# Adding two of a pair's three word tiles by DMA, with one list of tiles for words and exponentials

## The chip, the cores and the metric

The kernel runs on one core of one Trainium2 chip. The metric is the device time of one execution in microseconds; lower is better. Three runs of the kernel before gave 1370.07, 1371.21 and 1372.68 us, median 1371.21.

## What is computed

Two identical layers of a small transformer, on 2048 tokens of width 512, in bf16, with 32 heads of 16 columns. Each layer is attention and then a dense block with ReLU, each with a residual; the two layers share their weights.

```python
def _A_ref(x, wqkv, wo):
    ...
    scores = jnp.einsum("bhqd,bhkd->bhqk", q, k) * (Dh ** -0.5)
    p = _softmax(scores, axis=-1)
    o = jnp.einsum("bhqk,bhkd->bhqd", p, v)
    return (lambda x, *d: x.transpose(*d))(o, 0, 2, 1, 3).reshape(B, S, D) @ wo

def _B_ref(x, w1, w2):
    h = jnp.einsum("bsd,df->bsf", x, w1)
    ...
    return jnp.einsum("bsf,fd->bsd", h, w2)

x = A_x
x = x + _A_ref(_layernorm(x, axis=-1), A_wqkv, A_wo)
x = x + _B_ref(_layernorm(x, axis=-1), B_w1, B_w2)
x = x + _A_ref(_layernorm(x, axis=-1), A_wqkv, A_wo)
x = x + _B_ref(_layernorm(x, axis=-1), B_w1, B_w2)
```

The scores of both layers are 2 x 32 x 2048 x 2048 numbers, and each needs an exponential.

## The kernel before

**Slots.** A unit of work is 512 score columns: one head (or two or four blocks of keys, where fewer queries are taken), 128 keys on the partitions, queries along the columns. A slot takes W = 3 units. TensorE writes their scores into one of two PSUM tiles `ps_s` of three banks (L1946), and ScalarE turns them into exponentials in bf16, in an SBUF tile `e` (L1959). There are 1365 slots. The value matmuls (`pv`, L1299) multiply these tiles by the values `vaug`, which carry a column of ones for the softmax's denominator, and add up in PSUM `ps_o` or `ps_f`. They use 32 columns of the array each, so four heads run side by side; four such matmuls are called a round here. Between them TensorE does the projections and the dense block, the other matmuls (L429, L657, L666).

**Blocks on VectorE.** In some slots the third unit is not exponentiated by ScalarE, whose instruction then has 1024 columns and not 1536. VectorE evacuates it into the int16 tile `lin` (L1478): scores, a bias added and clamped, whose bits read as bf16 come near to an exponential. Two such blocks make a pair, 1024 columns. For a pair GpSimd makes two more tiles with a 64-bit integer add (L1533): `up` is lin plus a constant in each 16-bit word, `down` is lin minus it. The exponential is taken as lin + up + 1.55 x down. The sum is not formed: TensorE does three value matmuls, of lin and of up with `vaug`, and of down with `vscaled`, the values times 1.55 (for six blocks of keys; elsewhere VectorE weighs the down tile itself, L1537).

```python
            for part, buf, key, of in (
                ("lin", lin[which], line_key, None),
                ("up", up[p["n"] % NC], p["key"] + ("up",), None),
                ("down", down[p["n"] % ND], p["key"] + ("down",), p),
            )
```

So a block on VectorE costs TensorE three value matmuls, and a block on ScalarE one. Six tiles `lin`, three `up`, four `down` and five `e` of 1536 columns are taken in turn.

**The order.** Nothing is scheduled by the compiler. A loop over slots in the kernel's own program keeps a clock for each engine (`now_pe`, `now_dve`, `now_pool`, `exp_end`), with a cost for each kind of work, and writes the instructions of all engines in the order that follows: it picks the units of a slot, decides whether one goes to VectorE (`dve_block`, then `chain` for the pair), fills TensorE's time up to the next scores with value rounds (`fill_v`, `v_round`) and other matmuls (`fill_pe`), and repeats the scores where time is left. Engines then run their lists in order and wait on semaphores. The dictionary `rule` holds thresholds of these choices, `RULES` changes them at given slots, and `STARTS`, `MORE` and `SLIP` override single choices; these are "the table".

**Transfers.** SyncE (`SP`) issues nearly all DMAs: inputs, weights of the dense block (`load_w1`), transposes of the normalised rows (L796), the query tiles (L937) and the small ones of the softmax's denominators (L1191, L1195, L1243). GpSimd issues 46 DMAs that spread a denominator's rows over partitions (`widen`, L1253), and two loads at the start (L212).

Of the kernel before, what the change touches and what calls it, by code (L numbers as in the profile page):

```python
# [26 lines left out]
def kernel(  # L27
# [31 lines left out]
    NE = 5  # L59
# [13 lines left out]
    NP = 6  # L73
    NC = 3
    ND = 4
# [18 lines left out]
    STARTS, MORE, SLIP = {27: 0, 33: 0, 22: 0, 38: 1, 52: 0, 57: 0, 61: 0, 79: 0, 98: 0, 100: 1, 103: 1, 107: 1, 128: 1, 136: 0, 158: 1, 193: 0, 220: 1, 239: 0, 221: 0, 260: 1, 242: 1, 251: 0, 249: 0, 305: 1, 301: 1, 325: 1, 323: 1, 351: 0, 368: 1, 366: 0, 392: 1, 401: 1, 402: 0, 418: 0, 405: 1, 438: 1, 456: 0, 477: 1, 516: 0, 505: 1, 533: 1, 526: 0, 595: 1, 659: 0, 642: 0, 681: 0, 693: 0, 710: 0, 708: 0, 740: 1, 753: 0, 755: 1, 746: 0, 749: 0, 769: 0, 765: 1, 799: 1, 806: 0, 815: 1, 830: 1, 838: 0, 829: 0, 869: 1, 866: 0, 873: 1, 880: 0, 883: 0, 881: 1, 907: 1, 902: 0, 953: 0, 960: 0, 985: 0, 991: 0, 1026: 0, 1046: 0, 1068: 0, 1079: 0, 1067: 1, 1076: 1, 1096: 0, 1128: 0, 1125: 0, 1126: 0, 1156: 0, 1158: 0, 1178: 1, 1164: 0, 1189: 0, 1254: 1, 1280: 0, 1370: 0}, {8: 1.0, 2: -1.0, 15: -1.0, 28: 2.0, 42: -1.0, 80: 2.0, 72: -1.0, 95: 1.0, 92: 1.0, 87: -1.0, 156: 1.0, 166: -1.0, 207: 2.0, 223: 2.0, 234: -1.0, 287: 2.0, 318: -1.0, 407: 1.0, 437: 2.0, 495: -1.0, 486: 2.0, 520: 2.0, 533: 1.0, 564: 1.0, 572: 2.0, 577: 1.0, 594: -1.0, 589: 2.0, 599: -1.0, 620: 2.0, 624: 2.0, 649: -1.0, 660: 2.0, 643: 2.0, 669: -1.0, 683: -1.0, 712: 2.0, 736: 2.0, 735: 2.0, 738: 1.0, 741: 2.0, 758: 2.0, 757: 1.0, 786: 2.0, 784: 1.0, 814: 2.0, 819: 1.0, 839: 1.0, 861: 1.0, 874: 1.0, 865: -1.0, 886: 1.0, 897: 1.0, 892: 2.0, 953: 2.0, 955: 1.0, 941: 1.0, 1000: -1.0, 1022: 2.0, 1028: 2.0, 1033: 1.0, 1061: 1.0, 1119: -1.0, 1117: -1.0, 1112: 1.0, 1181: 1.0, 1205: -1.0, 1220: 1.0, 1221: -1.0, 1241: -1.0, 1255: -1.0, 1250: -1.0, 1276: 2.0, 1281: -1.0, 1326: 1.0, 1335: 2.0, 1357: 2.0, 1341: 2.0, 1347: 2.0}, {54: 216.0, 82: -200.0, 141: 216.0, 168: -200.0, 176: 120.0, 180: -200.0, 194: 120.0, 221: 120.0, 249: 120.0, 241: 216.0, 247: 60.0, 279: 120.0, 278: -200.0, 277: 216.0, 282: 216.0, 309: 120.0, 329: 120.0, 355: 216.0, 377: 120.0, 409: 120.0, 432: 120.0, 524: -200.0, 547: 216.0, 552: 216.0, 544: 120.0, 580: 216.0, 616: 60.0, 612: -200.0, 603: -200.0, 644: 60.0, 722: 120.0, 723: -200.0, 730: 60.0, 777: 120.0, 766: 60.0, 763: 60.0, 784: 216.0, 785: -200.0, 792: 216.0, 803: 60.0, 815: 60.0, 819: -200.0, 835: -200.0, 825: 216.0, 830: -200.0, 887: -200.0, 918: -200.0, 909: 216.0, 903: 216.0, 946: 216.0, 951: 120.0, 958: -200.0, 991: 60.0, 1044: 216.0, 1042: -200.0, 1057: 120.0, 1069: 120.0, 1071: 216.0, 1073: 60.0, 1111: 60.0, 1159: 60.0, 1200: 120.0, 1187: 60.0, 1196: 216.0, 1216: 120.0, 1238: 60.0, 1298: 120.0, 1313: 60.0, 1315: -200.0, 1304: -200.0, 1344: 120.0, 1362: -200.0, 1373: 120.0, 1365: 120.0}  # L94
# [4 lines left out]
        "backlog": 3000.0, "soon": 1400.0, "calm": 9.0, "most": 50.0, "unit": 320.0, "fill": 3000.0,  # L99
        "rounds": 4, "partial": 3, "far": 3, "young": 3, "old": 5, "slack": 1300.0, "eager": 0,  # L100
        "haste": 2.0, "margin": 130.0,
    }
    RULES = {1: {'pressed': 5, 'young': 6}, 21: {'backlog': 4000.0}, 41: {'unit': 360.0, 'pressed': 3, 'hold': 4, 'over': 0.0, 'calm': 1.5, 'cap': 10.0, 'fill': 2000.0, 'rounds': 4}, 61: {'full': 3}, 81: {'unit': 280.0, 'cap': 6.0, 'late': 99.0, 'spare': 10}, 101: {'slack': 300.0, 'fill': 2000.0}, 121: {'margin': 160.0, 'most': 2.0}, 141: {'eager': 0, 'hold': 4, 'late': 3.0, 'rounds': 3, 'pressed': 5, 'margin': 130.0, 'over': 0.0, 'partial': 3}, 161: {'full': 2}, 181: {'full': 2, 'ahead': 3.0, 'calm': 2.0, 'pace': 1.5, 'unit': 320.0, 'partial': 3, 'least': 0.5, 'most': 2.0}, 201: {'far': 2, 'pressed': 3, 'most': 2.0, 'least': 0.5, 'easy': 1.2, 'calm': 3.0, 'near': 8, 'rounds': 4}, 221: {'spare': 20, 'ahead': 3.0, 'calm': 1.2, 'haste': 2.0, 'hold': 4, 'pace': 1.3, 'cap': 3.0, 'young': 4}, 241: {'hold': 4, 'most': 50.0, 'ahead': 5.0, 'haste': 3.0}, 261: {'pressed': 5}, 281: {'cap': 3.0, 'least': 1.0, 'margin': 100.0, 'full': 2}, 301: {'far': 3, 'late': 99.0, 'pressed': 4, 'cap': 3.0, 'backlog': 2200.0, 'calm': 9.0, 'eager': 1, 'unit': 360.0}, 321: {'backlog': 2200.0, 'far': 3, 'eager': 0, 'cap': 6.0, 'unit': 320.0, 'over': 60.0, 'calm': 2.0, 'spare': 14}, 361: {'easy': 1.0, 'late': 2.0}, 381: {'cap': 3.0, 'slack': 300.0}, 401: {'eager': 0, 'pace': 0.7}, 421: {'calm': 9.0, 'old': 4}, 441: {'partial': 2, 'cap': 6.0, 'calm': 1.0, 'fill': 3000.0}, 461: {'pressed': 5}, 481: {'easy': 2.0, 'rounds': 3, 'cap': 10.0, 'pace': 1.0}, 501: {'haste': 1.6, 'ahead': 1.0, 'slack': 300.0, 'least': 1.0}, 521: {'margin': 100.0, 'unit': 360.0}, 541: {'cap': 3.0}, 561: {'closing': 3, 'full': 4}, 581: {'young': 6}, 621: {'partial': 2, 'late': 4.0}, 641: {'ahead': 3.0, 'calm': 1.0}, 661: {'far': 4, 'backlog': 3000.0}, 681: {'calm': 1.2, 'soon': 2000.0, 'unit': 360.0, 'hold': 2, 'far': 2, 'easy': 1.2, 'eager': 1, 'full': 3}, 701: {'young': 4, 'hold': 4}, 721: {'least': 1.0, 'pace': 0.7, 'backlog': 4000.0, 'fill': 3000.0}, 761: {'hold': 2, 'full': 3, 'closing': 6, 'haste': 2.0}, 821: {'over': 120.0, 'partial': 4}, 861: {'pace': 1.5, 'rounds': 3}, 881: {'spare': 6, 'far': 4}, 901: {'backlog': 3000.0}, 941: {'young': 3, 'pace': 1.0, 'far': 4, 'backlog': 3000.0, 'slack': 800.0, 'late': 99.0, 'partial': 2, 'pressed': 5}, 981: {'far': 4, 'slack': 800.0}, 1021: {'ahead': 8.0, 'pace': 0.7, 'rounds': 4, 'near': 6, 'far': 2, 'late': 2.0, 'backlog': 1500.0, 'full': 2}, 1041: {'margin': 60.0, 'young': 4}, 1061: {'margin': 100.0}, 1101: {'old': 4}, 1121: {'rounds': 4}, 1161: {'late': 99.0}, 1201: {'unit': 360.0, 'most': 50.0, 'calm': 1.5, 'over': 200.0, 'full': 4, 'least': 0.5, 'closing': 0, 'cap': 10.0}, 1221: {'margin': 160.0}, 1241: {'calm': 9.0, 'unit': 320.0}, 1261: {'hold': 4}, 1281: {'over': 120.0, 'backlog': 2200.0, 'least': 1.0, 'late': 99.0}, 1301: {'pace': 1.0, 'least': 0.5}, 1321: {'pressed': 4, 'slack': 1300.0}, 1341: {'calm': 1.2, 'unit': 320.0, 'far': 2, 'fill': 2000.0}, 1361: {'slack': 1300.0}}
# [22 lines left out]
    def sb(shape, dt, name):  # L126
# [11 lines left out]
    x_t = [sb([P, D], BF16, f"x{tt}") for tt in range(NTT)]  # L138
# [3 lines left out]
    kt1 = sb([P, 2, QS], BF16, "ktp1_0")  # L142
    ktp = [
# [3 lines left out]
                kt1[:, j, :] if T == 0 and j < 2 else sb([P, QS], BF16, f"ktp1_{T}_{j}")  # L147
# [5 lines left out]
    va2 = [sb([P, 2, H // 2, PW], BF16, f"vaug0_{n}") for n in range((NKB - TPC) // 2)]  # L153
# [3 lines left out]
    ]  # L157
    vaug.append(
        [sb([P, H // 2, PW], BF16, f"vaug1_{kb}") for kb in range(NKB - TPC)] + vaug[0][NKB - TPC :]
# [11 lines left out]
    acc = [  # L171
        x[:].bitcast(FP32).rearrange("p a b -> p (a b)") for x in kt01 + kt2
    ] + [
        x[:].rearrange("p k h d -> p (k h d)")[:, 0 : 2 * QS].bitcast(FP32) for x in va2
    ]
# [339 lines left out]
    def do_task(t):  # L515
# [11 lines left out]
        for k in t["makes"]:  # L527
            if k not in made:
                mark(k, t["engine"])

    def run_act():

        for t in act_q:
# [358 lines left out]
    def v_group(l, kb):  # L892
        def fin(b):
            nc.vector.tensor_copy(out=v_out(l, kb), in_=v_in(b))
            mark(("v", l, kb))
            if l == 0 and kb in SCALED:
                scale_v(l, kb, [])
# [1297 lines left out]
```

## Time and profile before

| | |
|---|---|
| median of three runs | 1371.21 us |
| the profiled execution's own time | 1371.6 us |
| its span, first to last instruction | 1369.8 us |
| granted TensorE clock | 1.000 |
| exponentials (L1959) of 1024 and 1536 columns | 1200 and 165 |
| evacuations of blocks on VectorE (L1478) | 1200, busy 802.4 us |
| adds on GpSimd (L1533) | 1200, busy 735.7 us |

The profile shows one execution. PE is TensorE's matmuls, PEld its weight loads, DVE VectorE, ACT ScalarE, POOL GpSimd, SP SyncE; a name that ends in q is that engine's sequencer. Busy times are in us, the mean of one instruction in ns. A group's line gives source line, engine, operation, tiles written and read, shape and count, then the busy time and mean, then the idle time of the engine just before these instructions and what ended most of it. A line of the waits reads: who waited, for whom, us in total, times, the longest. A line of transfers ends with the median us from issue to landing.

### The profile page before, as it was taken

The numbers are of one execution on the slowest core, as the hardware profiler recorded it, in microseconds if no ns is written. First come the engines' busy times: TensorE is split into PE (matmuls) and PEld (weight loads), VectorE is DVE, ScalarE is ACT, GpSimd is POOL, SyncE is SP. The second block draws the span as 40 slices with busy tenths as digits, with TensorE's granted clock in tenths as the row PEclk, the third lists the DMA queues.
The fourth block names the chain that finished last, engine by engine and source line by source line (L and its number), as shares of the span: only waits on it lengthen the run. The fifth ranks groups of instructions, "written<-read, shape, count | busy, mean of one in ns | idle before, by whom it ended". The sixth has DMA issues, their size and how long they took to land. (4 is left out here: it accounts for less than half of the span.)

```text
span 1369.8 us, 48788 instructions
## 1 busy us (share of the span) xinstructions
PE 1333.9 (97%) x20647; PEld 470.5 (34%) x20647; DVE 1145.0 (84%) x1994; ACT 1344.5 (98%) x1437; POOL 765.7 (56%) x1296
## 2 busy tenths in 40 slices
PE   8999999999999999999999999999999999999998
PEld 3222222222222222222222222222234444545665
DVE  7898998869998889986898877998988886887774
ACT  8999999999999999999999999999999999999995
POOL 3456666546566655664566544565545555565441
PEclk9999999999999999999999999999999999999999
DMA  6200012101022100210111100002112211214120
GB/s 148 70 2 14 21 43 45 47 16 33 11 49 48 23 21 6 56 42 18 25 21 32 33 5 6 11 15 52 41 35 51 50 28 38 65 30 96 35 58 19
DMA packets 151579, 50.03 MB, mean 37 GB/s; under 512 B 136608, under 2 KB 148576, under 8 KB 151360
## 3 DMA queue, kind: packets, MB, share of 16 engines
q1 hardware_dynamic: 144832, 41.31, 13.4%
q0 software_dynamic: 5568, 5.15, 2.0%
q8 instruction: 161, 2.64, 0.8%
q10 hardware_dynamic: 960, 0.46, 0.1%
q14 instruction: 58, 0.48, 0.1%
HBM read 24.38 MB, written 2.10 MB: 19 GB/s over the span
## 5 line engine op out<-in xcount | busy, mean ns | idle before, releaser
L1959 ACT ACTIVATE e<-ps_s 128x1024 bf16<-128x1024 f32 (+1 forms) x1366 | 1330.2, 1172 | 6.9 <-PE ps_s L1946 5.1
L1478 DVE TENSOR_SCALAR lin<-ps_s 128x512 int16<-128x512 f32 x1200 | 802.4, 684 | 154.8 <-PE ps_s L1946 116.5
L1533 POOL INT64_ADD up<-lin x600 | 367.6, 617 | 425.6 <-DVE lin L1478 220.7
L1946 PE MATMUL ps_s<-q,ktp 32*128 32x512 bf16 (+2 forms) x5460 | 523.3, 321 | 12.5 <-ACT e L1959 7.6
L1533 POOL INT64_ADD down<-lin x600 | 368.1, 617 | 130.8 <-DVE lin L1478 46.8
L1946 PEld LDWEIGHTS <-ktp 32*128 32x128 bf16 x5728 | 166.5, 91 | 509.4 <-issue 501.1
L1299 PEld LDWEIGHTS <-vaug 128*32 128x32 bf16 x7338 | 178.6, 95 | 196.0 <-issue 167.1
L1299 PE MATMUL ps_o<-e,vaug 128*32 128x512 bf16 (+2 forms) x2094 | 201.3, 321 | 2.6 <-DVE ht L1163 0.8
L1299 PE MATMUL ps_f<-e,vaug 128*32 128x512 bf16 (+2 forms) x1922 | 198.3, 330 | 1.4 <-DVE q L914 0.8
L1299 PE MATMUL ps_f<-lin,vaug 128*32 128x512 bf16 (+2 forms) x766 | 113.8, 332 | 0.1
L1299 PE MATMUL ps_f<-down,vscaled 128*32 128x512 bf16 (+2 forms) x728 | 113.5, 329 | 0.0
L1299 PE MATMUL ps_f<-up,vaug 128*32 128x512 bf16 (+2 forms) x766 | 113.1, 332 | 0.0
L1299 PE MATMUL ps_o<-up,vaug 128*32 128x512 bf16 (+2 forms) x850 | 110.2, 322 | 0.0
L1299 PE MATMUL ps_o<-lin,vaug 128*32 128x512 bf16 (+2 forms) x850 | 105.6, 322 | 0.5 <-DVE ht L1161 0.3
L1299 PE MATMUL ps_o<-down,vscaled 128*32 128x512 bf16 (+2 forms) x798 | 104.7, 320 | 0.0
L1299 PEld LDWEIGHTS <-vscaled 128*32 128x32 bf16 x1526 | 66.8, 96 | 29.2 <-issue 22.0
L429 PE MATMUL ps_o<-w,ht 128*32 128x512 bf16 x896 | 75.4, 383 | 0.6 <-issue 0.5
L429 PE MATMUL ps_f<-w,ht 128*32 128x512 bf16 x784 | 64.5, 383 | 0.2 <-DVE r L1187 0.2
L429 PE MATMUL ps_f<-xnT,w 128*32 128x512 bf16 x688 | 56.6, 383 | 1.5 <-DVE xn L933 1.2
L429 PE MATMUL ps_o<-xnT,w 128*32 128x512 bf16 x656 | 54.1, 383 | 0.1
L429 PEld LDWEIGHTS <-ht 128*32 128x32 bf16 x1680 | 36.5, 95 | 42.8 <-issue 34.8
L429 PE MATMUL ps_o<-xnT,wkq 128*32 128x512 bf16 x496 | 42.7, 383 | 1.7 <-DVE ht L991 0.5
(181 smaller groups left out, 851.9 us busy)
## 6 DMA issues: line engine op xcount, KB each, us to landing
w<-in_B_w_dram SPq DMA_DIRECT2D x144, 128.0 KB
q<-xn SPq DMA_DIRECT2D x36, 64.0 KB
out_dram<-x SPq DMA_DIRECT2D x15, 128.0 KB
x<-in_A_x_dram SPq DMA_DIRECT2D x14, 128.0 KB
ktp<-in_B_w_dram SPq DMA_DIRECT2D x10, 128.0 KB
r<-u POOLq DMA_DIRECT2D x8, 128.0 KB, 4.6
u<-u POOLq DMA_DIRECT2D x8, 128.0 KB, 4.6
xnT<-xn SPq DMA_TRANSPOSE x55
```

Source lines behind the costliest of these rows:

```text
L429: nc.tensor.matmul(G["b"][cols], lhsT[:, cols], rhs, start=not G["begun"][g], stop=not G["cols"][g], tile_position=(0, 32 * g), skip_group ...
L1299: nc.tensor.matmul((ps_f, ps_o)[sg["bank"]][32 * g : 32 * g + 32, 0 : sg["w"]], values[:, 4 * sg["T"] + g, 2 * e : 2 * e + 32], rhs, start ...
L1478: first = nc.vector.tensor_scalar(out=lin[which][:, half * QS : (half + 1) * QS], in0=src, scalar1=EXP_BIAS, scalar2=THIRD, op0=ALU.add, o ...
L1533: nc.gpsimd.int64_add(words(out), words(line), by)
L1946: score = nc.tensor.matmul(b[:, a : a + sg["w"]], kt[32 * g : 32 * g + 32, kc : kc + P], q_home(sg["q"])[32 * g : 32 * g + 32, sg["e"], 0 ...
L1959: ex = nc.scalar.activation(out=eb[:, 0 : place[m]], in_=b[:, 0 : place[m]], func=ACTF.Exp, scale=1.0 / (LOG2E * UNIT),)
```

## The change

- A pair can be *joined*: GpSimd issues a DMA that adds the pair's lin tile to its up tile in place (bf16), and TensorE multiplies that sum and the down tile, two value matmuls a block and not three. Whether a pair is joined is decided by `joins`: where GpSimd's queue reaches no further ahead than `rule["join"]`. The built program has 380 such transfers for 629 pairs.
- lin, up and down tiles, and exponential tiles too, come from one list `words` of 16 tiles of 1024 columns, taken when a task is written and given back after the last reader; ScalarE writes most 1024-wide exponentials there, and keeps three 1536-wide tiles (`NE`) of its own. Up to seven slots may be pending (`MOST`) in place of five.
- Tiles that a stage does not need are lent to that list and taken back later: `w2`, `wo`, `wv` and the key half of `wkq`, rows of `x`, keys and values of the second layer before they exist. What was overwritten is loaded again by SyncE before use (35 loads of w2, 40 of wo, 8 of wv, 4 of x).
- The first layer's first queries go through their keys in another order of runs, one matmul at the start is left out, and the table is new.

```diff
-    NE = 5
+    NE = 3
...
-    NP = 6
-    NC = 3
-    ND = 4
+    NWORDS = 16
+    X_BACK, W2_BACK, WO_BACK = 15, 5, 15
+    MOST = 7
...
+    JOINING, ADDED = 950.0, 3900.0
+    JOIN = {}
...
-    STARTS, MORE, SLIP = ...
+    STARTS, MORE, SLIP = ...
...
-    lin = [sb([P, GROUP * QS], I16, f"lin{n}") for n in range(NP)]
-    up = [sb([P, GROUP * QS], I16, f"up{n}") for n in range(NC)]
-    down = [sb([P, GROUP * QS], I16, f"down{n}") for n in range(ND)]
+    words_two = [sb([P, 2 * GROUP * QS], I16, f"words{n}") for n in range(NWORDS // 2)]
+    words = [
+        words_two[n // 2][:, n % 2 * GROUP * QS : (n % 2 + 1) * GROUP * QS] for n in range(NWORDS)
+    ]
+    free_words = list(range(NWORDS))
...
+    lent_w = [lend(wv[:, 2 * n : 2 * n + 2, :].rearrange("p c f -> p (c f)")) for n in range(2)]
...
+    lent_w2 = [
+        lend(w2[:, 2 * n : 2 * n + 2, :].rearrange("p a f -> p (a f)")) for n in range(NF // 2)
+    ]
...
-            steps = [(0, range(4), 0, TPC), (0, range(4), TPC, 2 * TPC), (0, range(4), 2 * TPC, NKB)]
+            steps = [(0, range(4), 0, TPC), (0, range(MID), TPC, 2 * TPC)]
+            steps += [(0, range(MID), 2 * TPC, NKB), (0, range(MID, 4), TPC, NKB)]
...
+    def take_e(full, by):
+
+        ready = [
+            k for k in free_words if k not in unclean and at([("words", k)], "act") <= by
+        ]
+        if full or len(free_e) > rule["wide"]:
+            if free_e:
+                return ebuf[free_e[0]][:], (), free_e.popleft()
...
+            elif ended_now:
+                loans.remove(x)
+                for n, k in enumerate(x["ks"]):
+                    def load(x=x, n=n):
+                        x["load"](n)
+                        mark(x["key"] + (n,), lag=sp_lag(W1, n=2) + 600.0)
+
+                    retire(k, load)
...
         for sg, kb, g in taken:
-            sg["rem"][g] += len(PARTS) - 1
+            sg["rem"][g] += len(PARTS) - 1 - p["joined"]
...
+            for part, key, of in (
+                ("lin", line_key, None),
+                ("up", p["key"] + ("sum" if p["joined"] else "up",), None),
+                ("down", p["key"] + ("down",), p),
+            )[p["joined"] :]
...
+    def joins(sg):
+        queued = sum(t["cost"] for t in pool_q)
+        early = max(now_pool[0] + queued, now_pe[0] + rule["fill"]) - now_pe[0]
+        return JOIN.get(slot[0], int(early < rule["join"] and sg["left"] >= rule["room"]))
...
+        def add():
+            ins = nc.gpsimd.dma_start(
+                out=of("up").bitcast(BF16), in_=of("lin").bitcast(BF16), accum_op=ALU.add
+            )
+            p["by"]["up"].append(ins)
+            mark(key + ("sum",), "pool", ADDED)
+
+        if p["joined"]:
+            task(JOINING, add, [key + ("sum",)], [key + ("up",)], engine="pool")
+            maker[key + ("sum",)].update(chain=p, late=300.0)
...
-        while len(pend) == NE:
-            force_v()
+        full_e = place[m] > GROUP * QS
+        home = None
+        while home is None:
+            home = take_e(full_e, max(exp_end[no - 1], now_pe[0] + PE_TO_ACT)) if len(pend) < MOST else None
+            if home is None:
+                force_v()
+        eb, ks, wide_e = home
```

In the changed kernel the same steps stand on other lines: scores L2216, exponentials L2234, value matmuls L1407, evacuations L1735, adds L1796, the joining transfer L1815, weighing L1801, other matmuls L466.

More of the change, by code (lines that the diff above doesn't have):

```diff
@@ L529, in do_task @@
                 mark(k, t["engine"])
+        if t["engine"] == "pool" and "chain" in t:
+            t["chain"]["issued"] += 1
+            settle(t["chain"])
     def run_act():
@@ L537, in run_act, with pool_ready @@
                 return
+    def pool_ready(t):
+        when = at(t["deps"], "pool")
+        if when is None or "takes" in t and not may_take(t["chain"]):
+            return None
+        when += t.get("late", 0.0)
+        return max(when, words_at("pool")[0]) if "takes" in t else when
     def run_pool(until):
         while now_pool[0] < until:
-            can = [(max(at(t["deps"], "pool"), now_pool[0]), n) for n, t in enumerate(pool_q)
-                   if at(t["deps"], "pool") is not None]
+            can = [(pool_ready(t), n) for n, t in enumerate(pool_q)]
+            can = [(max(when, now_pool[0]), n) for when, n in can if when is not None]
             if not can or min(can)[0] >= until:
@@ L863, in k_group @@
             k_mms(T, j), lambda b: k_fin(l, T, j, b), [("k", l, T, j)],
-            each(TPC, "xnT", ("ln1", l, j)) + [("wkq", T)],
+            each(TPC, "xnT", ("ln1", l, j)) + [("wkq", T)]
+            + [("gone", k) for k in (lent_k[j][T // 2] if l and j == 2 else lent_k[j][0] if l and j == 1 and T > 1 else None,) if k is not None],
         )
@@ L899, in v_group @@
         return mm_group(
-            v_mms(kb), fin, [("v", l, kb)], each(TPC, "xnT", ("ln1", l, kb // TPC)) + [("wv",)],
+            v_mms(kb), fin, [("v", l, kb)],
+            each(TPC, "xnT", ("ln1", l, kb // TPC)) + [("wv",)]
+            + [("ones", kb // 2)] * (l == 1 and kb // TPC in (1, 2))
+            + [("wv", kb // TPC, n) for n in range(2)] * (l == 1),
             cost=EVAC_V,
@@ L1397, in v_round @@
             grid_column(g)
-        while pend and not pend[0]["blocks"]:
-            pend.popleft()
+        for s in [s for s in pend if not s["blocks"]]:
+            pend.remove(s)
+            give_e(s)
         for p in list(pairs):
@@ L1402, in v_round @@
                 continue
-            for part in PARTS:
-                if ("free", part, p["n"]) not in made and not any(x[6] == part for x in p["mms"]):
-                    mark(("free", part, p["n"]), "pe")
-            for half in range(GROUP):
-                line = ("line", p["n"], half)
-                if ("read",) + line not in made and not any(x[4] == line for x in p["mms"]):
-                    mark(("read",) + line, "pe")
+            settle(p)
             if not p["mms"]:
@@ L1468, with words_at, take_words, may_take @@
     pairs = deque()
+    def words_at(engine):
+        return min((at([("words", k)], engine), n) for n, k in enumerate(free_words))
+    def take_words(p, part, engine):
+        when, n = words_at(engine)
+        k = free_words.pop(n)
+        del made["words", k]
+        p["tiles"][part] = k
+        return when
+    def may_take(p):
+        if not free_words:
+            return False
+        for q in pairs:
+            if q is p:
+                return True
+            if q["issued"] < 2:
+                return len(free_words) > 2 - q["issued"]
+        return True
@@ new lines, in gone, with give_words, retire @@
+    def gone(k, engine, when):
+        made["gone", k] = engine, when
+        if retiring[k]:
+            back.append((when, retiring[k]))
+    def give_words(k, engine, when):
+        if k in retiring:
+            gone(k, engine, when)
+        else:
+            made["words", k] = engine, when
+            free_words.append(k)
+    def retire(k, then=None):
+        retiring[k] = then
+        if k in free_words:
+            free_words.remove(k)
+            gone(k, *made.pop(("words", k)))
@@ new lines, with settle @@
+    for j in range(NQS):
+        loan(
+            lent_w[:2],
+            [("v", int(j > 0), kb) for kb in (range((j - 1) * TPC, j * TPC) if j else range(NKB))],
+            is_made("z", 0, j, 0), load_wv, ("wv", j),
+        )
+    def settle(p):
+        if len(p["blocks"]) < GROUP:
+            return
+        left_of = {x[6] for x in p["mms"]}
+        for part in list(p["tiles"]):
+            if part in left_of or (part == "lin" and p["issued"] < 2 + p["joined"]):
+                continue
+            engine, when = ("pool", now_pool[0]) if part == "lin" else ("pe", now_pe[0])
+            if part == "lin":
+                if p["joined"]:
+                    engine, when = made[p["key"] + ("sum",)]
+                elif now_pe[0] > when:
+                    engine, when = "pe", now_pe[0]
+            k = p["tiles"].pop(part)
+            touched.setdefault(k, deque(maxlen=20)).extend(p["by"][part])
+            (unclean.add if part == "lin" else unclean.discard)(k)
+            give_words(k, engine, when)
@@ L1760 @@
     now_pool[0] = POOL_READY
+    for j in (1, 2):
+        for k in lent_k[j] + lent_v[j]:
+            give_words(k, "pool", 0.0)
     sp_free[0] = 15500.0
     pair_at = None
-    def lin_free(n, half):
-        return n <= 0 or (
-            ("read", "line", n, half) in made
-            and all(("e", n, of) in made for of in ("up", "down"))
-        )
     def in_turn(x):
@@ L1980 @@
             )
-        exps[no % NE].append(ex.ins)
+        if wide_e is not None:
+            exps[wide_e].append(ex.ins)
+        for k in ks:
+            for earlier in touched.get(k, ()):
+                tc.declare_no_dep(
+                    ex.ins, earlier.ins,
+                    reason="the matmuls that read the buffer between the two writes order them",
+                )
         recent = recents[no % 2]
@@ L1997 @@
         run_act()
+        lend_and_take()
+        if lent_sums and all(("ot", 1, j, n // TPC, n % TPC) in made for j in range(2) for n in range(NT // 2 * TPC)):
+            while lent_sums:
+                give_words(lent_sums.pop(), "dve", now_dve[0])
         if to_load and no >= (FIRST_LOAD if len(to_load) > NF - KEPT_Q else LATER_LOAD) and sp_free[0] < now_pe[0]:
```

234 lines of the change are left out of this document (186 added, 48 removed).

## The prediction

> **What bounds the kernel now.** I read the page's first and fourth parts, the stretches of time, the groups by form, the waits, and last what GpSimd's own transfers cost. First the busy time of each engine and the chain's shares:
>
> ```profile
> PE 1333.9 (97%) x20647; PEld 470.5 (34%) x20647; DVE 1145.0 (84%) x1994; ACT 1344.5 (98%) x1437; POOL 765.7 (56%) x1296
> ...
> PE 28%; ACT 13%; DVE 4%; issue 1%; DMA 1%; POOL 0%; DVEq 0%; POOLq 0%
> ```
>
> TensorE and ScalarE both look full. Two stretches (busy us of PE, PEld, DVE, ACT, POOL; clock; DMA share; GB/s), and the exponential's two shapes:
>
> ```profile
> 400.00:500.00 100.00, 99.64 (x1272) 27.98 (x1264) 83.64 (x136) 100.00 (x108) 61.78 (x104) 1.00 0.13 28
> 500.00:600.00 100.00, 99.06 (x1259) 27.80 (x1252) 92.00 (x155) 100.00 (x110) 62.54 (x103) 1.00 0.18 37
> ```
> ```profile
> L1959 ACT ACTIVATE e<-ps_s 128x1024 bf16<-128x1024 f32 x1200 | 1123.1, 1124 | 4.0 <-PE ps_s L1946 3.5
> ...
> L1959 ACT ACTIVATE e<-ps_s 128x1536 bf16<-128x1536 f32 x165 | 240.9, 1524 | 2.8 <-PE ps_s L1946 1.6 <-PE ps_o L1299 0.4 <-PE ps_f L1299 0.4
> ```
>
> ScalarE is busy without a gap: 1365 exponentials, one per slot, 1330.2 us busy together, under 7 us of idle before them. TensorE's 97% counts overlapping matmuls. From the chain in order of time, twelve 512-wide column matmuls take 0.76 us and twenty take 1.19:
>
> ```profile
> 1350.13 0.76 PE ps_f L429 x12
> 1351.21 1.19 PE ps_f L429 x20
> ```
>
> So four of them, a round, stream in (1.19 - 0.76) / 2 = 0.215 us. A slot on average is 1345 / 1365 = 0.985 us. It holds one round of scores and about 2.2 others: per 512 columns, value matmuls 6496 / 4 = 1624 rounds, other matmuls near 1336. That streams in 0.69 us, and the timeline shows about 0.1 us at each of two changes of kind (the next matmul 0.32 us after the scores instead of 0.215), together some 0.9 us. Both engines lie close; ScalarE is the fuller, and TensorE ends last mainly where it hands scores over.
>
> **The change.** Counts come from the two built programs' instruction lists; durations from the profile.
>
> *Exponentials.* Both kernels have 1365 slots. 1024-wide ones go from 1200 to 1258, 1536-wide from 165 to 107: 58 more blocks of 512 leave ScalarE. The rows give 1524 - 1124 = 400 ns each, so 23.2 us. The other end: 1330.2 us over 1.482 million columns is 0.459 us per 512, 26.6 us, but that spreads fixed cost over columns. I take 23.2.
>
> *TensorE.* Of 629 pairs, 380 are joined: one value matmul on lin + up replaces two. The 58 further blocks cost two or three each instead of one. Per 512 columns value matmuls fall from 6496 to 5852, 161 rounds, 34.6 us less. Score columns rise by 48 matmuls (16 repeated rounds, 3.4 us), which the loop writes only into spare time. So TensorE is relieved by 31 to 35 us, more than ScalarE: the gain is capped by ScalarE, and TensorE gets more slack.
>
> *VectorE.* 58 more evacuations at 802.4 / 1200 = 0.669 us are 38.8 us; ten more weighings at 0.48 us 4.8; four fewer additions of partial sums -2.7; small others -0.8. So 1145 becomes 1185, 88% of 1348. Its fullest stretch goes from 92% to about 97%. Cover: 116.5 us of its idle time waited for scores. I cost it at nothing; gone, it costs the rival below.
>
> *GpSimd.* 58 more adds at 0.613 us are 36 us. The 380 issues are new. Nearest rows (min/median/max ns), transfers of 64 rows and of 512 short runs:
>
> ```profile
> L1253 POOL DMA_DIRECT2D r<-u x14: 616/628/643, 233.7 to 1205.1; - x14
> ...
> DMA to landing us min/median/max: 3.0/4.5/5.5
> ```
> ```profile
> L212 POOL DMA_DIRECT2D w<-in_A_wqkv_dram x2: 757/911/1065, 2.4 to 3.5; - x2
> ```
>
> A joined transfer has 128 rows of 2 KB, so 0.63 to 0.91 us: 239 to 346 us, and GpSimd reaches 1041 to 1148 us, 77 to 85%. A joined pair takes it 1.9 to 2.1 us; pairs come every 1348 / 629 = 2.14. Off the bound, but queued behind each issue (which waits for its own add) are the next pair's two adds and the 46 spreading transfers of L1253, and TensorE waits for those.
>
> *Landing.* This decides. The rows:
>
> ```profile
> r<-u POOLq DMA_DIRECT2D x8, 128.0 KB, 4.6
> ...
> r<-u POOLq DMA_DIRECT2D x6, 64.0 KB, 3.1
> ```
>
> A join moves 256 KB. Equal to the larger row, 4.6 us; going on by 1.5 us per doubling, 6.1; by 1.5 us per 64 KB, 7.6. Those rows read four source rows each, while a join reads all 128, so I expect less than the slopes say, 3 to 5 us. In the changed program the first matmul on a sum comes 9 slots or fewer after the pair's second block in 30 of 380 pairs, 10 in 85, 11 in 66, 12 or more in 199: 8.9, 9.9, 10.8 us at 0.985. Before the landing come handoff 0.2, evacuation 0.7, two adds 1.2, issue 0.9, and some 1.2 for another pair's adds: 4.2 us. A landing up to 4.7 us is hidden for nearly all.
>
> The Trainium skill (DMA: Bandwidth & Descriptors, "Anatomy of one DMA — SWDGE (gpsimd) path") gives about 2.0 us plus bytes / 436e3, by which 256 KB would land in 2.6 us, with no wait anywhere and the same sum. The 4.6 us row is far longer for half the bytes, and the page's fit does not speak of a read of the destination; so the rows keep the range.
>
> *The list of tiles.* The old fixed sets made GpSimd wait for TensorE:
>
> ```profile
> POOL up L1533 <- PE ps_f L1299: 93.2, 71, 4.8
> POOL up L1533 <- PE ps_o L1299: 88.5, 58, 5.5
> ```
>
> With the same for down, 260.7 us. One list shortens that, but GpSimd is not last: zero. It costs SyncE 87 reloads and 4 more query copies; its 128-row loads take 0.505 us to issue (middle value of L212 on SPq), so 91 x 0.5 = 46 us, behind which other SyncE transfers queue. Seven w2 reloads go out together (1.8 MB; the first 40 us moved 139 GB/s at share 0.60, so 232 at full share, 8 us), and nine groups of four rounds still stand ahead of their reader, some 18 slots. Zero; without cover 2 to 3 us in each of five chunks.
>
> Sum against the profiled execution, 1371.6 us (span 1369.8): 1371.6 - 23.2 = 1348.4; the median shown is 0.4 lower, so **1348 us**.
>
> **The rivals.**
>
> *Sums land late (slower).* From about 5.8 us landing the waits eat the gain. At 6.2 us a sum needs 10.4: 30 x 1.5 + 85 x 0.5 = 88 us of waits; a sum is due every 3.5 us, so about two flights share a stall: 44 us, 1392. For: the slopes above, and the software queue moved 5.15 MB in 2.0% of 16 engines' span, 85 us of one engine per MB, by which 380 joins are 39% of all DMA engines, twice that if reading the destination counts as much. Against: the four-row source. 1374 to 1450; chance 0.20.
>
> *Transfers crowd SyncE's.* The same engines carry transposes, weights and normalising rows. DMA is 1% of the chain, 14 us; doubled: 1362. For: the 39%. Against: DMA share is only 0.1 to 0.2 in the middle now. Chance 0.12.
>
> The same page ("Issuing engines are not separate DMA queues") says transfers share the 16 engines whoever issues them, which would give this 1362; no run here shows it yet.
>
> *TensorE's relief counts in full.* If TensorE's irregular hand-overs set the time, the whole 34.6 counts: 1371.6 - 34.6 = 1337. For: PE 28% against ACT 13% in the chain. Against: ScalarE without gaps. Chance 0.12.
>
> *VectorE takes the place.* Late evacuations hold the score banks and the 23 us are lost: about 1371. For: 97% in the fullest stretch. Against: 84% on average. Chance 0.06. That the change does not do what it says is excluded by the counts: 380 transfers that add, 918 fewer value matmuls.
>
> **How the numbers follow.** The forecast, 1341 to 1356, has 0.50. A difference under 0.2% (2.7 us) can't be told from none. Faster: 0.50 + 0.12 + 0.12 and a little of the last, 0.75; same 0.05; slower 0.20. The range 1334 to 1385 leaves out the long tail of late landings, some 0.15 to 0.18.
>
> **What would show it.** Right: about 1258 exponentials of 1024 with ScalarE still gapless; landing of the joins under 5 us; TensorE's idle time before matmuls on the lent tiles at a few us; GpSimd at 77 to 85%, VectorE at 88%. Wrong: landing over 5.8 us with TensorE, then ScalarE, idle; issues well over 0.9 us; VectorE above 95% throughout; waits on transposes or weights in the chain.

## The result and the profile after

The changed kernel takes **1425.27 us** (median of 3 runs, 1424.45 to 1429.75), against 1371.21 before: a ratio of 1.040, with a 95% interval of 1.0365 to 1.0439. I forecast 1348, and 1334 to 1385 as the range.

The first part of its page, the software queue (before: 2.0%), and the shares of the chain that ended last:

```profile
span 1422.7 us, 47537 instructions
...
PE 1339.9 (94%) x19774; PEld 461.0 (32%) x19776; DVE 1193.6 (84%) x2058; ACT 1332.0 (94%) x1437; POOL 1130.7 (79%) x1730
...
q0 software_dynamic: 60288, 104.79, 43.7%
...
PE 47%; ACT 25%; DVE 11%; DMA 10%; issue 4%; POOL 2%; SPq 0%; DVEq 0%; POOLq 0%; ACTq 0%
```

The two full engines are less full than before: TensorE went from 97% to 94%, ScalarE from 98% to 94%. VectorE stays at 84%, and GpSimd rises from 56% to 79%, so no other engine became the bound. The chain has changed: DMA was 1% of the span in it and is now 10%, 146 us by its pieces. The two shares do not cover the same ground: the shares of before add up to 47%, because that chain can be followed back to 732.5 us only, and its 11.6 us of DMA lie behind that point. The stretches that answer to those shown of before, and the worst one (busy us of PE, PEld, DVE, ACT, POOL; clock; DMA share; GB/s):

```profile
400.00:500.00 100.00, 99.41 (x1247) 26.51 (x1244) 87.03 (x138) 97.77 (x106) 91.52 (x139) 0.98 0.70 141
500.00:600.00 100.00, 92.90 (x1106) 25.20 (x1098) 85.53 (x145) 91.77 (x100) 84.29 (x129) 0.95 0.76 139
1000.00:1100.00 100.00, 87.80 (x1364) 31.42 (x1356) 72.09 (x131) 83.18 (x85) 68.56 (x102) 0.91 0.67 124
```

Two columns matter. The DMA share is four to over five times what it was (0.13 and 0.18 before, in the first two). The clock granted to TensorE, 1.00 in these stretches before, falls to 0.98, 0.95 and 0.91: where TensorE is stopped, it runs slower afterwards too.

The exponentials' largest groups, and the joins' landing times as the joining line's own view gives them:

```profile
L2234 ACT ACTIVATE e<-ps_s 128x1024 bf16<-128x1024 f32 x572 | 594.9, 1093 | 21.5 <-PE ps_s L2216 20.2 <-PE ps_f L1407 0.2
L2234 ACT ACTIVATE e<-ps_s 128x1536 bf16<-128x1536 f32 x98 | 141.9, 1490 | 20.7 <-PE ps_s L2216 20.2
```
```profile
L1815 POOL DMA_DIRECT2D words<-words x199: 842/1082/1339, 45.7 to 1380.4; - x199
...
DMA to landing us min/median/max: 3.2/4.0/8.3
```

Of ScalarE's gapless run nothing is left: 42 us of idle before these two groups alone, nearly all of it for scores. Landing is as expected, 4.0 us. The issue is not: its record lasts 1.08 us in the median (what it costs GpSimd is worked out further down).

**What a stall looks like.** The chain in order of time (start, length, what), at one of the places where TensorE stood, early in the second of these stretches:

```profile
512.83 6.03 DMA xnT<-xn
518.85 0.03 issue
518.88 0.05 DVEq L995
518.93 0.05 issue
518.98 0.70 DVE xn L995
519.68 0.04 issue
519.72 1.47 PE ps_o L1407 x11
```

A transpose of SyncE's (out of the tile xn) takes 6.03 us. VectorE's query step on L995 overwrites that tile, so it waits; it holds a bank of TensorE's, so TensorE waits. The timeline shows the same from TensorE's side, the idle time in brackets, with eight matmuls of one shape before the stall and behind it:

```profile
512.74 0.62 PE L466 MATMUL ps_o<-xnT,wkq 128*32 128x512 bf16 x8
...
519.72 0.61 PE L1407 MATMUL ps_o<-words,vaug 128*32 128x512 bf16 x1 [3.47 <-DVE xn L995]
...
521.67 1.04 PE L466 MATMUL ps_f<-xnT,wkq 128*32 128x512 bf16 x8
```

After 3.47 us of idle, what took 0.62 us takes 1.04. The granted clock in pieces of this stretch, in the column before the last two (a transfer's whole time counts in the piece where it starts, so the DMA share behind it can pass 1):

```profile
505.00:512.00 7.00, 6.03 (x58) 2.02 (x58) 6.05 (x11) 7.00 (x10) 5.72 (x10) 1.00 0.88 136
512.00:522.00 10.00, 6.22 (x65) 1.61 (x67) 5.21 (x9) 5.87 (x8) 7.96 (x13) 0.86 1.16 193
522.00:530.00 8.00, 8.00 (x85) 1.82 (x81) 6.13 (x11) 6.54 (x7) 5.30 (x9) 0.75 0.33 64
530.00:537.00 7.00, 6.95 (x93) 1.94 (x85) 6.87 (x11) 6.82 (x8) 5.15 (x9) 1.00 0.36 64
```

In the profiled execution TensorE was at half clock for 61 us, in 12 spells of 3.4 to 10.2 us; before, never.

### The profile page after: what moved, and what is told of

It reads as the page before. It is cut to its first block, busy times and chain, and to the rows that moved or that the text cites. A ratio compares the mean times of both kernels' runs of the same rounds, so it can differ in the third digit from the quotient of the medians.

```text
span 1422.7 us, 47537 instructions
## 1 busy us (share of the span) xinstructions
PE 1339.9 (94%) x19774; PEld 461.0 (32%) x19776; DVE 1193.6 (84%) x2058; ACT 1332.0 (94%) x1437; POOL 1130.7 (79%) x1730
## 3 DMA queue, kind: packets, MB, share of 16 engines
q0 software_dynamic: 60288, 104.79, 43.7%
## 4 chain that ended last, share of the span: by engine, by line
PE 47%; ACT 25%; DVE 11%; DMA 10%; issue 4%; POOL 2%; SPq 0%; DVEq 0%; POOLq 0%; ACTq 0%
PE ps_s L2216 17%; ACT e L2234 14%; PE ps_o L1407 8%; PE ps_f L466 7%; PE ps_f L1407 6%; PE ps_o L466 6%; DVE words L1735 4%; ACT w L2234 3%; DMA xnT<-xn 3%; ACT wv L2234 2%; ACT xx L2234 2%; DMA w<-in_B_w_dram 1%; ACT val L2234 1%; DMA words<-words 1%; ACT ktl L2234 1%
## 5 line engine op out<-in xcount | busy, mean ns | idle before, releaser
L2234 ACT ACTIVATE e<-ps_s 128x1024 bf16<-128x1024 f32 (+1 forms) x670 | 731.1, 1151 | 42.2 <-PE ps_s L2216 40.4
L1735 DVE TENSOR_SCALAR words<-ps_s 128x512 int16<-128x512 f32 x924 | 616.9, 684 | 95.5 <-PE ps_s L2216 76.0
L1796 POOL INT64_ADD words<-words x683 | 507.4, 856 | 140.0 <-DVE words L1735 105.9
L2216 PE MATMUL ps_s<-q,ktp 32*128 32x512 bf16 (+2 forms) x4142 | 496.0, 336 | 18.7 <-ACT e L2234 5.5
L2216 PEld LDWEIGHTS <-ktp 32*128 32x128 bf16 x4418 | 153.7, 91 | 464.1 <-issue 454.3
L2216 PE MATMUL ps_s<-q,ktl 32*128 32x256 bf16 (+2 forms) x1358 | 206.1, 292 | 3.4 <-DVE words L1735 1.7
L1815 POOL DMA_DIRECT2D words<-words x199 | 200.3, 1006 | 0.8 <-POOL words L1796 0.4
L1407 PEld LDWEIGHTS <-vaug 128*32 128x32 bf16 x4298 | 116.6, 95 | 172.7 <-issue 151.0
L2234 ACT ACTIVATE w<-ps_s 128x1024 bf16<-128x1024 f32 x145 | 148.9, 1069 | 7.9 <-PE ps_s L2216 7.4
L1407 PE MATMUL ps_o<-e,vaug 128*32 128x512 bf16 (+2 forms) x903 | 137.3, 343 | 0.8 <-DVE u L1263 0.3
L2234 ACT ACTIVATE wv<-ps_s 128x1024 bf16<-128x1024 f32 x110 | 118.6, 1084 | 5.0 <-PE ps_s L2216 4.8
L2234 ACT ACTIVATE vaug<-ps_s 128x1024 bf16<-128x1024 f32 x114 | 116.5, 1046 | 4.1 <-PE ps_s L2216 3.7
L1407 PE MATMUL ps_f<-e,vaug 128*32 128x512 bf16 (+2 forms) x669 | 106.4, 348 | 1.5 <-DVE ktp L914 1.0
L2234 ACT ACTIVATE xx<-ps_s 128x1024 bf16<-128x1024 f32 x93 | 103.2, 1124 | 2.5 <-PE ps_s L2216 2.5
L1407 PE MATMUL ps_o<-words,vaug 128*32 128x512 bf16 (+1 forms) x552 | 95.3, 372 | 5.0 <-DVE xn L995 3.5
L1407 PE MATMUL ps_o<-words,vscaled 128*32 128x512 bf16 (+2 forms) x598 | 92.2, 328 | 0.2 <-DVE ht L1054 0.2
L1407 PE MATMUL ps_f<-words,vscaled 128*32 128x512 bf16 (+2 forms) x546 | 86.6, 331 | 0.4 <-issue 0.4
L2216 PEld LDWEIGHTS <-ktl 32*128 32x128 bf16 x1358 | 63.7, 92 | 58.4 <-issue 56.6
L1407 PEld LDWEIGHTS <-val 128*32 128x32 bf16 x2094 | 67.3, 96 | 39.3 <-issue 30.7
L466 PE MATMUL ps_f<-w,ht 128*32 128x512 bf16 x952 | 77.3, 382 | 1.1 <-DVE q L976 0.5
L1407 PEld LDWEIGHTS <-vscaled 128*32 128x32 bf16 x1554 | 66.1, 96 | 29.0 <-issue 22.6
L1407 PE MATMUL ps_f<-words,vaug 128*32 128x512 bf16 (+1 forms) x360 | 66.3, 376 | 0.8 <-DVE ht L1239 0.8
```

What stands on the lines that cost most here:

```text
L466: nc.tensor.matmul(G["b"][cols], lhsT[:, cols], rhs, start=not G["begun"][g], stop=not G["cols"][g], tile_position=(0, 32 * g), skip_group ...
L1407: nc.tensor.matmul((ps_f, ps_o)[sg["bank"]][32 * g : 32 * g + 32, 0 : sg["w"]], values[:, 4 * sg["T"] + g, 2 * e : 2 * e + 32], rhs, start ...
L1735: first = nc.vector.tensor_scalar(out=words[which][:, half * QS : (half + 1) * QS], in0=src, scalar1=EXP_BIAS, scalar2=THIRD, op0=ALU.add, ...
L1796: ins = nc.gpsimd.int64_add(of(part).bitcast(I64), of("lin").bitcast(I64), by)
L1815: ins = nc.gpsimd.dma_start(out=of("up").bitcast(BF16), in_=of("lin").bitcast(BF16), accum_op=ALU.add)
L2216: score = nc.tensor.matmul(b[:, a : a + sg["w"]], kt[32 * g : 32 * g + 32, kc : kc + P], q_home(sg["q"])[32 * g : 32 * g + 32, sg["e"], 0 ...
```

## The experiments

The theory: the joins' bytes fill the DMA engines, so transfers that SyncE issues (transposes, weights, normalising rows) land late; TensorE, and then ScalarE, stop for them, and each stop is made longer by the half clock behind it. The main rival: the sums themselves are late. Others: the reloads; GpSimd's longer work; the plan. Another, that the traffic slows the engines themselves, does not fit the two profiles: an evacuation on VectorE takes 684 ns in both, and a narrow exponential back to back 0.916 to 0.917 us on both chains. Each ratio, with its 95% interval, is to the kernel before as it ran beside that experiment (medians 1370.64 to 1372.42 us). "After" is the changed kernel, 1425.3 us. Its three times spread over 5 us, so a difference of some 5 us against it is at the edge of what can be told.

**Few bytes.** Each of the 380 transfers carries 64 bytes of each row in place of 2 KB.

```diff
-out=of("up").bitcast(BF16), in_=of("lin").bitcast(BF16), accum_op=ALU.add
+out=of("up")[:, 0:32].bitcast(BF16), in_=of("lin")[:, 0:32].bitcast(BF16), accum_op=ALU.add
```

> The changed kernel with every joining transfer cut to 32 of its 1024 columns (so sums are wrong in the rest); every engine's list of instructions keeps its order. Theory A (the bytes of the joins crowd SyncE's transfers on the DMA engines, TensorE runs dry, and each stall is followed by a stretch at half clock): most of the loss goes, 1345 to 1370 us, clock near 1.00, DMA out of the chain. Rival B (GpSimd's time for the issues and its slower adds): as the changed kernel, 1415 to 1430. Rival C (SyncE's reloads) and rival D (the new order itself): also 1410 to 1430.

Measured: 1374.98 us, 1.0034 [1.0022, 1.0046]. Queue and chain:

```profile
q0 software_dynamic: 60288, 8.29, 8.6%
...
PE 55%; ACT 29%; DVE 10%; issue 3%; DMA 3%; SPq 0%; DVEq 0%; POOL 0%; ACTq 0%
```

So 50.3 us hang on the bytes, with every instruction in its place.

**No transfer.** The issue in `add()` is left out; the order stays.

> The changed kernel with the 380 joining transfers left out, all else in the same order (sums are wrong). Theory A: a little under the kernel with few bytes, 1340 to 1365. Rival B: 1340 to 1365 here only, and not with few bytes. C and D: still 1410 to 1430.

Measured: 1356.56 us, 0.9898 [0.9879, 0.9918]; GpSimd is busy 807.7 us. Another 18.4 us go with the transfers themselves.

**No reload.** The 87 reloads of lent weight tiles are left out.

```diff
 def load(x=x, n=n):
-    x["load"](n)
     mark(x["key"] + (n,), lag=sp_lag(W1, n=2) + 600.0)
```

> The changed kernel without the loads that bring back lent tiles (w2, wo, wv, rows of x: what is multiplied there is wrong), all else in the same order. Theory A: the joins stay, so 1405 to 1425. Rival C: 1345 to 1370. Rival D: 1415 to 1430.

Measured: 1391.61 us, 1.0149 [1.0133, 1.0166]. The chain's DMA share falls from 10% to 5%: beside the joins the reloads cost 33.7 us.

**Neither transfers nor reloads.** The last two edits together.

> The changed kernel without joining transfers and without reloads (sums and reloaded weights are wrong), order kept. If reloads hurt only in the crowd that the joins make: within 5 us of the kernel without transfers, 1350 to 1357. If they cost by themselves: 1325 to 1340.

Measured: 1353.29 us, 0.9872 [0.9859, 0.9886], and ScalarE is full again:

```profile
PE 1307.1 (97%) x19774; PEld 458.0 (34%) x19776; DVE 1174.1 (87%) x2058; ACT 1322.5 (98%) x1437; POOL 808.3 (60%) x1350
...
PE 48%; ACT 42%; DVE 8%; issue 2%; DMA 0%; SPq 0%; DVEq 0%; ACTq 0%
```

Without the joins the reloads cost 1356.6 - 1353.3 = 3.3 us, with them 33.7. (The intervals of the two runs just touch, so 3.3 may be less or nothing.) They hurt mainly in the joins' crowd. This is nearly the 1348 that I forecast: the sum comes close for a kernel without these transfers.

**Few bytes, copied.** As with few bytes, but the transfer copies and does not add.

```diff
-    out=of("up")[:, 0:32].bitcast(BF16), in_=of("lin")[:, 0:32].bitcast(BF16), accum_op=ALU.add
+    out=of("up")[:, 0:32].bitcast(BF16), in_=of("lin")[:, 0:32].bitcast(BF16)
```

> All 380 joining transfers carry 32 of 1024 columns, as in the run with few bytes, but copy instead of adding (the sums are left out). That run took 1375.0 us; with no transfers at all 1356.6, so 18.4 us hang on something other than the bytes. Theory GpSimd: the adding transfer takes about 1.0 us to issue and lengthens the adds beside it from 0.62 to 0.86 us; a copy took 0.56 us and left them at 0.62. Then most of the 18.4 us come back: 1358 to 1364 us, with GpSimd busy near 915 us instead of 1130. Rival: 380 landings, each some 2 us late, and their small rows on the DMA engines cost it, whoever issues them: then the copy takes 1371 to 1376 us as the adding one did.

Measured: 1369.54 us, 0.9985 [0.9974, 0.9995]. GpSimd's two groups in this kernel:

```profile
L1796 POOL INT64_ADD words<-words x683 | 415.3, 618 | 173.2 <-DVE words L1735 138.0 <-ACT w L2234 9.9 <-PE ps_f L1407 7.5
L1815 POOL DMA_DIRECT2D words<-words x199 | 110.8, 557 | 0.0
```

With few bytes added, the records of the same adds lasted 861 ns and those of the issues about 1 us. Of the 18.4 us only 5.4 go with adding against copying, which includes GpSimd's 134 us of longer work and the small rows' own share (8.6% against 3.2% of the DMA engines). The other 13.0 come with 380 transfers of any kind; how much of it is GpSimd's time for them (188 us more than without transfers) and how much their landings, no run separates. Neither theory holds whole; both expectations missed.

**Whole copy.** All bytes, copied and not added (`accum_op` dropped).

> The changed kernel with every joining transfer a plain copy of the same 256 KB (the up tile is overwritten and not added to), order kept. If adding costs the DMA engines more than moving (a 2 KB row took 193 ns in the changed kernel, where a 1 KB row of SyncE's took 50), a row falls to about 90 ns, the software queue's share from 44% to about 20%, and by theory A the time to 1385 to 1405. If bytes alone count: 44% and 1420 to 1430.

Measured: 1381.41 us, 1.0063 [1.0043, 1.0083]:

```profile
q0 software_dynamic: 35968, 104.79, 21.9%
...
PE 51%; ACT 30%; DVE 9%; DMA 6%; issue 3%; POOL 0%; SPq 0%; DVEq 0%; ACTq 0%
```

The same 2 KB rows take half the engines' time if they are not added to something. Full copies cost 11.9 us more than small ones; full adds cost 50.3 more than small adds. So the crowd's cost is not proportional to the share it takes.

**Half the joins small.** Every second transfer carries 32 of 1024 columns.

> The changed kernel with every second joining transfer cut to 32 columns, order kept. Theory A with a cost in proportion: half way between few bytes (1375) and all (1425), 1395 to 1405. If a crowd only matters above some load: 1375 to 1390.

Measured: 1389.34 us, 1.0139 [1.0113, 1.0165], at a queue share of 26.6%. Half the bytes give back 35.9 of the 50.3 us: the second half costs more than twice the first.

**Sums not awaited.** TensorE reads a fixed tile in place of each sum, so it never waits for one; transfers and everything else stay.

> The changed kernel with all 380 joining transfers at full size, but TensorE reads a fixed tile where it read their sums, so it waits for none of them (the value matmuls on sums are wrong); order of instructions kept. Theory A (the joins' bytes delay SyncE's transfers): 1395 to 1420, most of the loss stays, with transposes and weights in the chain. Rival L (the joins' own sums land late, as the prediction had it): 1370 to 1380, as with few bytes.

Measured: 1420.63 us, 1.0349 [1.0331, 1.0366]. Late sums cost 4.6 us by the medians, 7 by the two ratios, and hardly over 13 by their intervals, of the 72 that joins and reloads cost together. The rival falls as the main cause.

**Reloads small.** The 87 reloads carry 32 columns each; the joins stay whole.

> The changed kernel with all 87 reloads cut to 32 columns (what is multiplied there is wrong), joins at full size, order kept. If the reloads cost by their bytes on the DMA engines: as without reloads, 1385 to 1400. If by their issue time on SyncE's queue: as the changed kernel, 1415 to 1430.

Measured: 1398.44 us, 1.0200 [1.0185, 1.0216]. Of the reloads' 33.7 us, 26.8 hang on their bytes and 6.8 on what is left of them, 87 issues and as many rows as before, of 64 bytes each.

**No joins.** `joins()` returns 0, so the planner makes another order, with the new table but without a join: 1228 narrow exponentials, 137 wide, and no value matmuls saved by sums. Then the same without reloads.

> The changed kernel with no pair joined (the plan is then another: three value matmuls for every block on VectorE), with the list of tiles, the lending and the new table kept. Theory A: clock 1.00 and no stalls on transfers; TensorE's relief is gone, so about the kernel before or a little slower, its table not being made for this, 1370 to 1390. Rival C (reloads): 1400 or more. Rival D: 1400 or more.

> The kernel without joins (1403.9 us), with its reloads of lent weights left out as well (their data are then not the weights). Theory: 33 us over the kernel before come from its plan and its three value matmuls for every block, and reloads without joins are nearly free (3.3 us in the run with neither): 1398 to 1402 us. Rival: the reloads stall TensorE here too, through SyncE's queue: then 1370 to 1385 us.

Measured: 1403.86 us, 1.0233 [1.0213, 1.0253], and without reloads 1400.27, 1.0215 [1.0197, 1.0232]. The clock is 0.998 and the DMA 1% of the chain, so little is crowded; the reloads cost 3.6 us here, with intervals that overlap. The remaining 29 us over the kernel before belong to the plan or to the value matmuls that are not saved; the table was not made for this, and the two are not told apart. The 1356.6 us of the run without transfers lie 47 us lower, while the transfers that make the sums take 68.7. That the 47 are the matmuls saved by joining is not shown: the two plans differ in 30 blocks on VectorE as well, which alone put 30 x (1.343 - 0.916) = 12.8 us on ScalarE, by the exponentials' times given below.

**Later due times.** The planner reckons with longer transfers (transposes 4.5 us, small ones 2.9, weights 4.4, sums 4.6), which gives another order; then also w2 and wo are not lent.

```diff
+SMALL, W1, TRANSPOSE = (600.0, 2900.0), (390.0, 4400.0), (1260.0, 4500.0)
+JOINING, ADDED = 950.0, 4600.0
```

> The changed kernel with the plan's landing times set to what the changed trace showed: transposes 4.5 us after issue, small transfers 2.9, weights 4.4, sums 4.6 (before: 2.4, 1.45, 2.4, 3.9). The plan becomes another (1226 narrow exponentials, 369 joins), with a table made for the old one. Theory A: fewer stalls, clock 0.99 or more, 1375 to 1405. If the stalls are not from late transfers: 1425 or more.

> The same landing times, and w2 and wo are not lent, so 75 of the 87 reloads are gone (1218 narrow exponentials, 362 joins). Theory A, with the reloads' bytes as part of the crowd: below the kernel with the lags alone, 1360 to 1390. If reloads matter only by SyncE's issue time or not at all: as the kernel with the lags alone.

Measured: 1426.53 us, 1.0391 [1.0370, 1.0411], and 1422.86, 1.0363 [1.0340, 1.0386]. Both are misses: planning for longer landings gained no time. Half clock fell from 61 us to 44 and 31, so there was less of that, and the time did not follow. Both have a new order with a table made for another: with 1226 and 1218 narrow exponentials the least time for all of them, worked out below, is 14 and 17 us longer. Their chains can be followed over 28% and 56% of the span only, and what else was lost stays open.

**Twelve stalls forced on the kernel before.** At slots 150, 250 and so on to 1250, TensorE waits for a small transfer which waits for the last exponential.

```diff
+if no % 100 == 50 and 100 < no < 1300:
+    nc.sync.dma_start(out=pause[:], in_=ebuf[(no - 1) % NE][:, 0:P])
+    nc.tensor.matmul(b[:, 0:P], pause[:], pause[:], start=True, stop=True)
```

> The kernel before, with twelve stalls put into TensorE: at every hundredth slot from 150 to 1250 a small DMA copies a piece of the slot before's exponentials, and one more matmul waits for it ahead of the scores. Each should idle ScalarE some 2 to 3 us. If a stall only costs its own idle time, the kernel is 25 to 40 us longer with the clock at 1.00. If each is followed by a stretch of 3.4 us or more at half clock, as in the changed kernel's trace, the clock reads under 0.99 and the cost is 45 to 80 us.

Measured: 1426.18 us, 1.0393 [1.0366, 1.0420]. One of the waits, and the stretches around it:

```profile
663.33 0.23 PE L1944 MATMUL ps_s<-pause 128*128 128x128 bf16 x1 [2.47 <-DMA pause<-e]
```
```profile
655.00:660.00 5.00, 5.00 (x70) 1.37 (x62) 4.98 (x9) 5.00 (x7) 3.90 (x8) 1.00 0.05 19
660.00:663.00 3.00, 0.86 (x11) 0.13 (x11) 1.13 (x2) 1.58 (x2) 1.54 (x3) 1.00 0.22 69
663.00:668.00 5.00, 4.67 (x41) 1.06 (x41) 2.30 (x4) 2.74 (x3) 0.67 (x2) 0.66 0.05 7
668.00:673.00 5.00, 5.00 (x71) 1.54 (x72) 3.44 (x6) 5.00 (x6) 1.77 (x3) 1.00 0.28 53
```

The stall itself lengthens its slot by 2.5 to 4.2 us, 35.5 in all; the eleven slots behind each stall lose some 21 more in all. All twelve are followed by 3.4 or 6.8 us at half clock (58.0 in all), and TensorE is busy 25 us longer than in the kernel before (1358.9 against 1333.9). The kernel loses 55 us: a stall costs about 1.6 times its own length. So a dozen short stalls make a loss as large as this change's, with the DMA engines little used (1.9% by GpSimd's queue, 12.9% by the hardware queue).

The Trainium skill (TensorE: Matmul & The Clock Gate, "Part 1: The HAM clock gate") says that the clock falls to half after an idle window of about 3.4 us and rises after a busy one. The pieces of 3.4 us agree with its window. But ten of the twelve waits, 2.45 to 2.88 us long, were shorter than the idle window it asks for, and the clock halved behind each of them.

## Why the prediction was wrong

**Where the 1425.3 us come from**, by the runs that keep the order:

| step | median us | difference |
|---|---|---|
| after | 1425.3 | |
| the joins' bytes down to a 32nd | 1375.0 | -50.3 |
| copied, not added | 1369.5 | -5.4 |
| no transfers | 1356.6 | -13.0 |
| no reloads either | 1353.3 | -3.3 |

The last step is 33.7 instead where the joins are there: the two costs hang together.

**Exponentials: right.** 58 blocks left ScalarE (1258 narrow, 107 wide). Back to back a narrow one takes 0.916 us on the chain and a wide one 1.343. So the least time for all falls from 1200 x 0.916 + 165 x 1.343 = 1320.8 to 1258 x 0.916 + 107 x 1.343 = 1296.0, by 24.8; I took 23.2, with 26.6 as the other end. What lies above this floor in the span grew from 49.0 us to 126.7, and is 55.2 with neither transfers nor reloads. The 5 us between 1353.3 and my 1348 were not looked into.

**VectorE and TensorE: right in size.** VectorE is busy 1193.6 us (1185 forecast). TensorE's relief shows where nothing stalls it: 1307.1 busy against 1333.9, 27 us, though a busy TensorE counts overlap. None of it mattered.

**GpSimd: right, though an issue looks longer.** 1130.7 us lie in 1041 to 1148. An issue's record lasts 1.0 us on average, over my upper end of 0.91, and an add's 0.86 in place of 0.62. But the two overlap; the next pair's adds start some 0.6 us into the issue:

```profile
513.79 1.12 POOL L1815 DMA_DIRECT2D words<-words  x1
514.40 1.76 POOL L1796 INT64_ADD words<-words  x2
```

By busy time an adding transfer costs GpSimd (1130.7 - 807.7) / 380 = 0.85 us, inside my 0.63 to 0.91, and a copy (996.2 - 807.7) / 380 = 0.50. The nearest rows were copies. At most 5.4 us of the result hang on adding against copying with few bytes.

**Landing: right, and not what decides.** I wrote "This decides", and gave 3 to 5 us with waits hidden up to 4.7. The median is 4.0, and not waiting for sums saves about 5 us. The rival "Sums land late" had the right sign, by a mechanism that carries about 5 us, not 44.

**The failed step: "Transfers crowd SyncE's", priced at 14 us doubled.** I had its mechanism and its cause (39% of all DMA engines' time by estimate, 43.7% measured), gave it 0.12, and priced it by what DMA was of the chain before, 14 us. The runs show 50.3 us for the joins' bytes alone, and 72.0 for all joining transfers and reloads. Even the 14 us were misread: they are 1% of the whole span, but the chain of before covers only its last 635 us, so the first half was left out. And doubling has no ground: they are what was late at a share of 0.1 to 0.2, and say nothing of what becomes late at 0.7. In the profile after, SyncE's transfers are about 109 us of the chain: transposes 37, the rows of the denominators 38, weights 22, queries 9, the first load 3 (added up from the pieces that the chain lists). The sums' own are 29, and GpSimd's spreading transfers 8. Some of SyncE's pieces, with their lengths:

```profile
681.32 6.12 DMA xnT<-xn
...
994.34 11.91 DMA w<-in_B_w_dram
...
1027.23 5.42 DMA u<-c
...
1123.02 7.08 DMA q<-xn
```

The chain of the run without transfers lists two transfers over 2 us, one of them the first load. The chain of before lists such transfers too (a transpose of 4.31 us, a weight load of 3.80); I asked only which engine was full, not how much later each could land.

Two prices were missing in that step. The first is what follows a stall. Beside the run with neither transfers nor reloads, which has the same 19774 matmuls and no half clock, TensorE is idle 38.7 us longer (82.8 against 44.1, span less busy time) and busy 32.8 us longer (1339.9 against 1307.1); half of its 61 us at half clock is 30.7. So of the 71.5 us between the two spans more than two fifths are slower matmuls and not waiting. By the forced stalls it is some 0.6 us for each us of stall. The second is the adding: the read of the destination, which I named ("twice that if reading the destination counts as much"), does count. A row takes (43.7% - 2.0%) x 16 x 1422.7 us / 48640 rows = 195 ns if added and (21.9% - 2.0%) x 16 x 1375.1 / 48640 = 90 ns if copied. My 39% came out only by chance: it took 85 us of one engine per MB from the transfers of before, while these, as copies, take 0.199 x 16 x 1375.1 / 99.64 MB = 44, and adding doubles it.

**The list of tiles: costed at zero, with 2 to 3 us in each of five chunks if the cover is gone.** Without joins that nearly holds: 3.3 and 3.6 us. With them it is 33.7. The two edits were priced each by itself, against a DMA that was nearly idle; the price lies in their meeting.

The Trainium skill (DMA: Bandwidth & Descriptors, "Issuing engines are not separate DMA queues") says that transfers run on the same 16 DMA engines and interleave, whichever engine issued them. The traces agree: with GpSimd's queue at 43.7%, SyncE's transfers land late. By the fit that the Trainium skill gives on the same page ("Anatomy of one DMA — SWDGE (gpsimd) path"), 256 KB would take an estimated 2.6 us. The whole copy landed in 2.7; the adding transfer took 4.0, which the fit does not cover.

## What to carry to other kernels

Price a background transfer not only by when it lands, but by what it does to every transfer that has a waiter: list those with their slack, before giving a queue a large share of the DMA engines. Price edits that use the same resource together, and a stall of TensorE by more than its length (1.6 times here). Where a sum can be made by a transfer that adds, count its rows twice (195 ns against 90 here), and its time on GpSimd as well.

## What the runs showed of the hardware

- A transfer that adds a 2 KB row within SBUF takes 195 ns of a DMA engine, a copied row 90; with 64 bytes it is (8.6% - 2.0%) x 16 x 1376.0 / 48640 = 30 ns against (3.2% - 2.0%) x 16 x 1364.3 / 48640 = 5 ns.
- Such a transfer keeps GpSimd busy 0.85 us longer than none, a copy 0.50, whatever the bytes (1130.7 and 1130.4 us of busy time, and 996.6 and 996.2, against 807.7). The record of the adding issue lasts 1.0 us against 0.56, and that of the 128x1024 adds around it, which begins inside it, 0.86 against 0.62. Why was not tried.
- TensorE's clock halved for 3.4 or 6.8 us after each of twelve waits of 2.45 to 3.81 us, 2.75 on average.
- A crowd's cost rises faster than its share: 1375.0, 1389.3 and 1425.3 us at queue shares of 8.6%, 26.6% and 43.7%.
